# A planned attention and two-MLP kernel: who takes the head's maximum and the slope, which banks attention may use, and when the second weights are fetched

## The chip, the cores and the metric

The kernel runs on one core of a Trainium2 chip. The time is device microseconds of one execution. Three runs of the kernel before gave 874.43, 874.75 and 878.87 us; the median is 874.75 us. The engines have short names here: PE multiplies matrices (TensorE), DVE is VectorE, ACT is ScalarE, POOL is GpSimd, and SP issues most of the DMAs.

## The reference

Four batches of eight heads, 576 tokens and 64 dimensions go through linear attention with exponential features; the result, 2304 tokens by 512, goes through two MLPs of width 2048.

```python
def phi(x):                                   # x = q or k, scaled; omega is 128 x 64
    h = einsum('bhsd,md->bhsm', x, omega) - sum(x * x) / 2
    return exp(h - max(h, axis=-1)) / sqrt(m)
kv = einsum('bhsm,bhsd->bhmd', phi(k), v);  z = sum(phi(k), axis=2)
attn = einsum('bhsm,bhmd->bhsd', phi(q), kv) / (einsum('bhsm,bhm->bhs', phi(q), z) + 1e-6)
x = attn, heads side by side                  # 2304 x 512
h = x @ moe_w_in                              # 512 -> 2048
x = (maximum(h, 0) + alpha * minimum(h, 0)) @ moe_w_out
h = x @ moe2_w_in
x = where(h >= 1, h, where(h <= -1, 0, (h + 1)**2 / 4)) @ moe2_w_out
```

The term with x * x is the same for all features of a token, so the maximum that is subtracted takes it out again.

## The kernel before, in words

All work is written as Python generators. A planner (`Plan`, L38) runs them while the kernel is built: each step names an engine, a cost in ns and the instruction; where a step is a list, `_choice` (L105) takes the engine on which it would end first by the planner's costs, plus a handicap that the list may give. The step that can start first is emitted next. So the order on every engine is fixed when the program is built, and each engine goes through its queue in that order. Tokens stand for buffers and PSUM banks; a generator that asks for one waits until another gives it back.

Attention goes by pairs of heads: 16 pairs, four to a batch. For a pair, `features` (L527) multiplies keys and queries by omega into two PSUM banks, and `exponentials` (L503) takes for each head of a pair the maximum over the features on DVE and then the exponentials on ACT, in one of two ways. Either ACT runs one instruction of 128 columns for each of the four token blocks, with the maximum as its bias (L523); or DVE first subtracts the maximum from all 512 columns (L514), which frees the bank, and ACT runs one instruction of 512 columns (L516). In the kernel before, the second head of keys and of queries of pairs 0 to 5 (`N_SUB = 6`) goes the second way. `transposed` turns the query features on PE, `key_sums` forms kv, and the quotients end with a multiplication on POOL for the main 512 tokens and one for the remaining 64 (L805).

The first MLP works on batches 0 to 2 in 48 units, 16 of 128 hidden features for each batch. A unit is twelve matmuls of 512 columns into a hidden bank (h0 or h1), the slope, a split of the result into a high and a low part (`hi_of`, `lo_of`, L275 and L282), and twelve matmuls into the output banks y0 to y3. The order on PE is hidden of unit i + 1, then output of unit i, and attention of the later batches stands between. Before the first unit, batch 0 of attention must be done (four pairs) and x split; PE fills planned gaps of 600 ns and more there with matmuls on zeros (L1819, called fills here). Until the first hidden matmuls are in the queue, attention uses the banks y0 to y3, a0 and a1; then only a0 and a1.

The slope (L924 to L930) is two DVE instructions: t = min(h, 0) * alpha, then h = max(h, 0) + t, both reading the hidden bank. The weights arrive as 64 bit floats and are converted in five steps on ACT or POOL, ACT, DVE, DVE and POOL (`convert`, L311); then a high and a low part is made (`split`, L481): the high part on ACT, the low part by a subtraction on POOL or DVE. The second MLP's weights are fetched from unit 14 on (`W2_FROM`). From 376 us on the first MLP's last batch and the second MLP run in Strassen-like form, which the change does not touch.

Of the kernel before, what the change touches and what calls it, by code (L numbers as in the profile page):

```python
# [146 lines left out]
def _act(n, emit, more=0.0):  # L147
    return "act", 100 + 0.833 * n + more, emit


def _dve(n, emit, handicap=0.0):
    return "dve", 65 + 1.05 * n, emit, handicap
# [27 lines left out]
def favor_attention_two_mlps(  # L180
# [20 lines left out]
    nc = tc.nc  # L201
# [16 lines left out]
    NR = GT // P  # L218
    K2 = KC // 2
    AHEAD = 5  # L220
    N_SUB = 6
    SQ = 32
    BY_SQUARES = range(6, 16)
    ZW = 32
# [2 lines left out]
    WARM = 18  # L227
    WARM_NS = 125
    W2S = 4, 5
    W2_FROM = 14  # L230
    FRESH = 10
    SPLIT_EARLY = 4
    PACE = 0
# [31 lines left out]
    def ev(*key):  # L265
        return events.setdefault(key, Event())

    def done(*key):
        plan.set(ev(*key))
# [211 lines left out]
    def split(both, w):  # L481
        hi, lo = both[:, 0, :], both[:, 1, :]
        yield hi_of(hi, w, 3000)
        yield lo_of(lo, w, hi, ("pool", "dve2"), 600)


    free_banks = Tokens(["y0", "y1", "y2", "y3", "a0", "a1"])
    xs_of_pair, v_slots, split_slot = Tokens([0, 1]), Tokens([0, 1]), Tokens([0])
    k_slot = Tokens([0, 1])
    q_slot = Tokens([0])  # L490
# [6 lines left out]
    def give(tag):  # L497
        if tag[0] == "a" or not started:
            plan.put(free_banks, tag)
        else:  # L500
            plan.put(y_banks, tag)

    def exponentials(pool, pr, tag, dst, key):  # L503

        n = dst.shape[1]


        pv = pr[:, : n * M].rearrange("p (n m) -> p n m", m=M)
        nm = pool.tile([P, 4], F32, tag="nm", name="nm", bufs=8)[:, :n]
        yield _dve(n * M, lambda: nc.vector.tensor_reduce(nm, pv, AX.X, ALU.max, negate=True))  # L510
        if key[0] in ("k1", "q1") and key[1] < N_SUB:

            most = nm.unsqueeze(2).to_broadcast([P, n, M])
            yield _dve(n * M, lambda: nc.vector.tensor_tensor(dst, pv, most, ALU.add))  # L514
            give(tag)
            yield _act(n * M, lambda: nc.scalar.activation(dst, dst, AF.Exp), 10)  # L516
            done(*key)
            return
        for i in range(n):
            src = pv[:, i, :]  # L520
            if len(dst.shape) > 3:
                src = src.rearrange("p (c t) -> p c t", t=SQ)
            yield _act(M, lambda: nc.scalar.activation(dst[:, i], src, AF.Exp, bias=nm[:, i : i + 1]), 40)  # L523
        give(tag)
        done(*key)

# [244 lines left out]
    def inverted(pair):  # L771
        b, hp = divmod(pair, NP)
        den, num, inv, sums = backs[pair]
        yield ev("den", pair)
        squares = den.rearrange("p (s j) -> p s j", j=32)
        halves = inv.rearrange("p (i s) -> p i s", i=2)

        def add():
            nc.vector.tensor_scalar(sums, squares[:, NS // 2 :, 0], EPS, None, ALU.add)

        def invert():
            nc.vector.reciprocal(halves, sums.unsqueeze(1).to_broadcast([P, 2, NS // 2]))
# [12 lines left out]
        if pair in BY_SQUARES:  # L795
            o, a, r = ends[0]
            a, r = (e.rearrange("p (r j t) -> p r j t", j=NJ, t=SQ) for e in (a, r))
            ends[0] = o.rearrange("p (j r t) -> p r j t", j=NJ, t=SQ), a, r
        for i, (o, a, r) in enumerate(ends):
            for p in range(2):  # L800
                yield ev("num", pair, p)
            n = a.free_size()
            yield [
                _dve_two(n, lambda: nc.vector.tensor_tensor(o, a, r, ALU.mult), 2000),
                _pool(n, lambda: nc.gpsimd.tensor_tensor(o, a, r, ALU.mult)),  # L805
            ]
        plan.put(den_slot, 0)
        done("pair", pair)

# [79 lines left out]
    def attended():  # L889
        for b in range(B):  # L890
            for hp in range(NP):
                yield ev("pair", b * NP + hp)
            if b < B - 1:
                done("x", 0, b)
        att.close()
        late["pool"] = ctx.enter_context(tc.tile_pool(name="late", bufs=1, reuse_waits="tile"))
        late["zero"] = late["pool"].tile([P, 512], F32R, name="zero")
        nc.gpsimd.memset(late["zero"].bitcast(F32), 0.0)
        for u in range(2):
            late["g", u] = late["pool"].tile([P, 2, GT], F32R, name=f"g{u}")  # L900
        done("late")
        done("x", 0, B - 1)
        done("x", 0, B)
# [5 lines left out]
    def split_x(b, c):  # L909
# [7 lines left out]
        xs[c] = hi, lo  # L917
        done("xs", b, c)

    t_slots = Tokens([0])  # L920
    g_slots = Tokens(["g0", "g1"])
    gs = {}

    def activate(i, h, tag):  # L924
        g, f = units[i]
        yield t_slots
        t = moe_p.tile([P, SM], F32, tag="t", name="t")
        a = alpha_sb[:, f : f + 1]
        yield _dve(SM + 57, lambda: nc.vector.tensor_scalar(t, h, 0.0, a, ALU.min, ALU.mult))
        yield _dve(SM, lambda: nc.vector.scalar_tensor_tensor(h, h, 0.0, t, ALU.max, ALU.add))  # L930
        plan.put(t_slots, 0)
        tg = yield g_slots
        both = moe_p.tile([P, 2, SM], F32R, tag=tg, name="g")
        g_hi, g_lo = both[:, 0, :], both[:, 1, :]
        yield hi_of(g_hi, h)
        yield lo_of(g_lo, h, g_hi)
        plan.put(h_banks, tag)
        gs[i] = g_hi, g_lo, tg
        done("g", i)

    h_banks = Tokens(["h0", "h1"])
    y_banks = Tokens([])

    def hidden(i, c, h):
# [22 lines left out]
    def first_mlp():  # L967
        ys = {}
        for i in range(-1, NU):
            if i + 1 < NU:  # L970
# [16 lines left out]
                if not started:  # L987
                    started.append(1)
                    for at, tag in list(free_banks.free):
                        if tag[0] == "y":  # L990
                            free_banks.free.remove((at, tag))
                            y_banks.free.append((at, tag))
                if i + 1 == NU - 1:
                    done("first hidden")
            if i < 0:
# [85 lines left out]

    def second_parts(m, j):
        if not m:
            yield ev("unit", NF + 7 * j // 2)
        for u in range(2):
            yield ev("w", m, 2 * j + u, 0)
        rank = NU + 2 * j if m else NF + 2 * j
# [704 lines left out]
    ident = const.tile([P, P], F32, name="ident")  # L1792
    alpha_sb = const.tile([P, NF], F32, name="alpha_sb")
    half = const.tile([P, 1], F32, name="half")

    ctx.enter_context(tc.manual_schedule())
    att = ExitStack()
# [59 lines left out]
        yield "act", 300, constants  # L1857

    plan.add(setup(), URGENT)
    plan.add(load(alpha_sb, alpha, ("alpha",)), 0)  # L1860
    for f in range(-AHEAD, 0):
        done("unit", f)
    plan.add(attend(pool), 3, -10)
# [74 lines left out]
```

## Time and profile before

| | |
|---|---|
| median of three runs | 874.75 us |
| span of the profiled execution, first to last instruction | 872.5 us |
| PE busy | 862.4 us, 99% |
| DVE busy | 746.8 us, 86% |
| ACT busy | 547.1 us, 63% |
| POOL busy | 257.0 us, 29% |
| granted clock | 0.999 of 2.4 GHz over the span |
| first hidden matmul of the first MLP | 52.30 us |
| end of the first MLP's plain units | about 376 us |

The busy time of PE counts each matmul until its result has drained, so rows overlap: a matmul of 512 columns is shown with 0.39 us, while the next one starts 0.23 us behind it. Whether PE is late is therefore read from the starts of its rows and from its waits, not from the 99%. The number in brackets at a row of the timeline is the idle time ahead of it and what ended it.

### The profile page before, as it was taken

What the parts mean: (1) busy time and instruction counts of PE and PEld (TensorE: products, weight loads), DVE (VectorE), ACT (ScalarE), POOL (GpSimd) and SP (SyncE); (2) the same over time, 40 slices, a digit from 0 to 9 for tenths busy, and PEclk for the clock granted to TensorE, in tenths of its full rate; (3) what the DMA queues carried; (4) which work ended last, traced back from release to release, by engine and by line L of the source; (5) the groups of instructions that cost most, each with busy time, mean ns of one, the idle gap of its engine ahead of it and who ended that gap; (6) DMA issues with size and microseconds to landing.
All of it is one profiled execution on the core that took longest, in us unless ns stands there. A gap on an engine that the chain in (4) does not pass through costs nothing.

```text
span 872.5 us, 17520 instructions
## 1 busy us (share of the span) xinstructions
PE 862.4 (99%) x6197; PEld 758.7 (87%) x6197; DVE 746.8 (86%) x1385; ACT 547.1 (63%) x1193; POOL 257.0 (29%) x230
## 2 busy tenths in 40 slices
PE   8999999999999999999999999999999999999998
PEld 7777777777777788889999999989999999999998
DVE  6998998998886989898999999765978998688964
ACT  6996776676767654344755666655567765476653
POOL 1665667566759876200112012100000000000000
PEclk9999999999999999999999999999999999999999
DMA  9869978589999767779877769978487788888773
GB/s 241 232 195 262 261 216 249 188 282 288 314 327 333 242 203 270 268 262 310 283 266 251 267 208 317 322 265 289 157 293 255 277 260 253 251 270 241 234 244 127
DMA packets 122791, 224.05 MB, mean 257 GB/s; under 512 B 41936, under 2 KB 60496, under 8 KB 122704
## 3 DMA queue, kind: packets, MB, share of 16 engines
q1 hardware_dynamic: 122400, 222.74, 78.9%
q8 instruction: 49, 0.80, 0.4%
q14 instruction: 38, 0.31, 0.1%
q10 hardware_dynamic: 304, 0.20, 0.1%
HBM read 163.13 MB, written 59.77 MB: 255 GB/s over the span
## 4 chain that ended last, share of the span: by engine, by line
PE 86%; DMA 6%; ACT 2%; DVE 2%; issue 1%; SPq 1%; POOL 1%; ACTq 0%; DVEq 0%; POOLq 0%
PE y L293 12%; PE y L294 11%; PE y L295 11%; PE h L293 11%; PE h L295 11%; PE h L294 11%; PE a L295 4%; PE a L294 4%; PE a L293 4%; DMA raw<-w 3%; PE a L544 2%; PE a L711 2%; PE a L648 1%; PE y L544 1%; POOL w L336 1%
## 5 line engine op out<-in xcount | busy, mean ns | idle before, releaser
L336 POOL TENSOR_TENSOR w<-w,raw 128x512 uint32<-128x512 uint32 x64 | 97.2, 1526 | 233.9 <-DVE w L335 201.6
L293 PE MATMUL h<-x_hi,w_set 128*128 128x384 f32 x288 | 97.2, 338 | 0.0
L295 PE MATMUL h<-x_hi,w_set 128*128 128x384 f32 x288 | 96.9, 336 | 0.0
L294 PE MATMUL h<-x_lo,w_set 128*128 128x384 f32 x288 | 96.8, 336 | 0.0
L293 PE MATMUL y<-g,w_parts 128*128 128x512 f32 x192 | 78.0, 406 | 0.0
L293 PE MATMUL h<-x_hi,w_parts 128*128 128x512 f32 x192 | 77.3, 403 | 0.0
L295 PE MATMUL h<-x_hi,w_parts 128*128 128x512 f32 x192 | 75.1, 391 | 0.5 <-POOL w_parts L288 0.5
L294 PE MATMUL y<-g,w_parts 128*128 128x512 f32 x192 | 75.0, 391 | 0.0
L295 PE MATMUL y<-g,w_parts 128*128 128x512 f32 x192 | 75.0, 391 | 0.0
L294 PE MATMUL h<-x_lo,w_parts 128*128 128x512 f32 x192 | 74.8, 390 | 0.0
L288 POOL TENSOR_TENSOR w_parts<-w,w_parts 128x512 fp32r<-128x512 f32 x40 | 53.4, 1335 | 21.2 <-ACT w_parts L277 18.9
L277 ACT ACTIVATE g<-h 128x512 fp32r<-128x512 f32 x48 | 28.7, 598 | 47.2 <-DVE h L930 47.2
L293 PEld LDWEIGHTS h<-x_hi,w_set 128*128 128x128 f32 x288 | 54.1, 188 | 3.8 <-ACT e L1330 0.3
L294 PEld LDWEIGHTS h<-x_lo,w_set 128*128 128x128 f32 x288 | 54.1, 188 | 3.3
L277 ACT ACTIVATE g<-gates 128x384 fp32r<-128x384 f32 x72 | 37.6, 526 | 30.6 <-PE y L294 10.6
L295 PEld LDWEIGHTS h<-x_hi,w_set 128*128 128x128 f32 x288 | 54.1, 188 | 0.0
L331 DVE SCALAR_TENSOR_TENSOR raw<-raw 128x512 uint32<-128x512 uint32 x64 | 50.6, 801 | 1.2 <-issue 0.8
L287 DVE TENSOR_TENSOR g<-gates,g 128x384 fp32r<-128x384 f32 x72 | 39.4, 552 | 13.9 <-ACT g L277 13.6
L277 ACT ACTIVATE w_parts<-w 128x512 fp32r<-128x512 f32 x58 | 36.6, 633 | 21.7 <-PE h L295 10.5
L293 PEld LDWEIGHTS y<-g,w_parts 128*128 128x128 f32 x192 | 36.1, 188 | 9.5 <-PE a L711 0.5
L294 PE MATMUL y<-g,w_out 128*128 128x512 f32 (+1 forms) x120 | 44.1, 367 | 0.0
L295 PE MATMUL y<-g,w_out 128*128 128x512 f32 (+1 forms) x120 | 43.9, 366 | 0.0
(248 smaller groups left out, 2709.0 us busy)
## 6 DMA issues: line engine op xcount, KB each, us to landing
w_set<-w_kept SPq DMA_DIRECT2D x56, 512.0 KB, 5.3
w_out<-w_kept SPq DMA_DIRECT2D x56, 512.0 KB, 4.3
raw<-w SPq DMA_DIRECT2D x48, 512.0 KB, 5.5
w_kept<-w_keep SPq DMA_DIRECT2D x72, 256.0 KB, 4.0
w_set<-w_kept SPq DMA_DIRECT2D x24, 768.0 KB, 4.4
w_again<-w_word SPq DMA_DIRECT2D x48, 256.0 KB, 3.6
w_kept<-w_keep SPq DMA_DIRECT2D x24, 512.0 KB, 5.1
kq<-kq SPq DMA_DIRECT2D x15, 576.0 KB, 5.2
```

The lines of the kernel that those rows point to most:

```text
L277: ops = [_act(n, lambda: nc.scalar.activation(hi, src, AF.Copy))]
L287: "dve2": _dve_two(n, lambda: nc.vector.tensor_tensor(*args), bias),
L288: "pool": _pool(n, lambda: nc.gpsimd.tensor_tensor(*args)),
L293: nc.tensor.matmul(out_, wh, mh, start=first, stop=False, skip_group_check=more)
L294: nc.tensor.matmul(out_, wh, ml, start=False, stop=False, skip_group_check=more)
L295: nc.tensor.matmul(out_, wl, mh, start=False, stop=last, skip_group_check=more)
L331: lambda: nc.vector.scalar_tensor_tensor(low, e, 0x80000000, low, ALU.bitwise_and, ALU.bitwise_or),
L336: yield _pool(n, lambda: nc.gpsimd.tensor_tensor(d, d, low, ALU.add))
L544: nc.tensor.matmul(o, x[rows, c], om[rows, :], start=True, stop=True)
L648: nc.tensor.matmul(o, kf[:, 2 * j + h, r], vm[:, h, j, :], start=False, stop=end)
L711: nc.tensor.matmul(o[r], weights[i], moving[i], start=True, stop=True)
```

## The change

- `exponentials`: which of the two ways a head goes is no longer fixed for the second heads of pairs 0 to 5, but chosen by the planner for every head of four token blocks of pairs 0 to 3 (`N_SUB = 4`), the way over ACT alone with a handicap of 200.
- `slope` (new): the first of its two instructions may run on ACT (t = relu(-h)); then DVE forms h = h + t * (1 - alpha). The old two DVE instructions remain as the other choice. The table 1 - alpha (`rest_sb`) is made once, on POOL.
- `split`: the low part of the weights is made by DVE alone.
- Bank h1 belongs to attention until the first hidden matmuls are in the queue, and to the hidden units after that.
- The second weights are fetched from unit 10, and their sums are formed from unit 16 + 3j instead of 16 + 3.5j.
- A batch of x may be split when the main multiplication of its last pair is in the queue, ahead of that for the remaining 64 tokens.

```diff
-    N_SUB = 6
+    N_SUB = 4
-    W2_FROM = 14
+    W2_FROM = 10
@@ split
-        yield lo_of(lo, w, hi, ("pool", "dve2"), 600)
+        yield lo_of(lo, w, hi, ("dve2",))
@@
-    free_banks = Tokens(["y0", "y1", "y2", "y3", "a0", "a1"])
+    free_banks = Tokens(["y0", "y1", "y2", "y3", "a0", "a1", "h1"])
@@ give
-            plan.put(y_banks, tag)
+            plan.put(y_banks if tag[0] == "y" else h_banks, tag)
@@ exponentials
-        if key[0] in ("k1", "q1") and key[1] < N_SUB:
-            most = nm.unsqueeze(2).to_broadcast([P, n, M])
-            yield _dve(n * M, lambda: nc.vector.tensor_tensor(dst, pv, most, ALU.add))
+        first = _act(M, lambda: one(0), 40)
+        if n == NJ and key[1] < N_SUB:
+            yield [(*first, 200), ("dve", 65 + 1.05 * n * M, take)]
+        else:
+            yield first
+        if taken:
             give(tag)
             yield _act(n * M, lambda: nc.scalar.activation(dst, dst, AF.Exp), 10)
@@ inverted
+            done("pair", pair, i)
@@ attended
-                yield ev("pair", b * NP + hp)
+                yield ev("pair", b * NP + hp, 0)
@@ activate
-        yield _dve(SM + 57, lambda: nc.vector.tensor_scalar(t, h, 0.0, a, ALU.min, ALU.mult))
-        yield _dve(SM, lambda: nc.vector.scalar_tensor_tensor(h, h, 0.0, t, ALU.max, ALU.add))
+        yield from slope(h, t, f)
@@ slope, new
+        def relu():
+            nc.scalar.activation(t, h, AF.Relu, scale=-1.0)
+        def leaky():
+            nc.vector.scalar_tensor_tensor(h, t, rest, h, ALU.mult, ALU.add)
+        yield [
+            (*_act(SM, relu), 0),
+            _dve(SM + 57, lambda: nc.vector.tensor_scalar(t, h, 0.0, a, ALU.min, ALU.mult)),
+        ]
+        if on_act:
+            yield _dve(SM + 57, leaky)
+        else:
+            yield _dve(SM, lambda: nc.vector.scalar_tensor_tensor(h, h, 0.0, t, ALU.max, ALU.add))
@@
-    h_banks = Tokens(["h0", "h1"])
+    h_banks = Tokens(["h0"])
@@ second_parts
-            yield ev("unit", NF + 7 * j // 2)
+            yield ev("unit", NF + 3 * j)
```

What the planner makes of it, counted over the whole program: of 48 units 41 take the slope's first step on ACT; of 12 heads that DVE subtracted before, 3 remain; the subtractions for w_parts<-w go from 40 on POOL and 18 on DVE to 58 on DVE; the fills go from 25 matmuls to 17, besides the 18 at the start. Besides that, a few conversions and sums change engines.

On PE, around the first hidden unit, the queue before reads as follows. The number behind a name tells buffers apart, the letter and digit ahead of it is the PSUM bank; warm_w is a fill, qf, kf, lf are features of a pair, qt and kvz the two operands of the quotients, and h0_1194 is unit 0.

```order
L1819 MATMUL h0_214<-warm_w_208 128x256 x8
L677 MATMUL y3_1107<-ident_196,qf_1022 128x128 x4
L711 MATMUL y0_1123<-qt_875,kvz_919 32x288 x4
L711 MATMUL a1_1122<-qt_875,kvz_919 32x512 x4
L711 MATMUL y0_1123<-qt_875,kvz_919 32x64 x4
L642 MATMUL y0_1123<-vl1_240,lf_876 32x130 x4
L648 MATMUL y0_1123<-vm1_239,kf_879 32x65 x32
L677 MATMUL y2_1190<-ident_196,qf_1022 128x128 x4
L293 MATMUL h0_1194<-x_hi_1114,w_parts_731 128x512
```

The same place now, from the last three matmuls of unit 0 (h0_1128) to the first three of unit 1 (h0_1238):

```order
L293 MATMUL h0_1128<-x_hi_1090,w_parts_599 128x512
L294 MATMUL h0_1128<-x_lo_1091,w_parts_599 128x512
L295 MATMUL h0_1128<-x_hi_1090,w_parts_599 128x512
L723 MATMUL h1_1158<-qt_895,kvz_964 32x288 x4
L723 MATMUL a0_1157<-qt_895,kvz_964 32x512 x4
L723 MATMUL h1_1158<-qt_895,kvz_964 32x64 x4
L654 MATMUL h1_1158<-vl1_241,lf_896 32x130 x4
L660 MATMUL h1_1158<-vm1_240,kf_900 32x65 x32
L689 MATMUL a1_1170<-ident_196,qf_1058 128x128 x4
L293 MATMUL h0_1238<-x_hi_1084,w_parts_918 128x512
L294 MATMUL h0_1238<-x_lo_1085,w_parts_918 128x512
L295 MATMUL h0_1238<-x_hi_1084,w_parts_918 128x512
```

Unit 0 stands ahead of the block of attention behind which it stood, the eight fills ahead of that block are gone, and units 0 and 1 use the same bank, since attention still has h1.

On ACT, the queue before around the high part of unit 0 (g_1322):

```order
L523 ACTIVATE kf_1211<-a0_1254,nm_1272 128x128
L523 ACTIVATE kf_1211<-y1_1255,nm_1273 128x128
L277 ACTIVATE g_1322<-h0_1194 128x512
L523 ACTIVATE kf_1211<-a0_1254,nm_1272 128x128
L523 ACTIVATE kf_1211<-y1_1255,nm_1273 128x128
```

And now, from ACT's last exponential ahead of the slope of unit 0 (t_1166) to its high part (g_1225); raw is a weight in conversion:

```order
L522 ACTIVATE qf_1058<-a1_1062,nm_1078 128x128
L327 ACTIVATE raw_1045<-raw_1045 128x512
L939 ACTIVATE t_1166<-h0_1128 128x512
L277 ACTIVATE w_parts_1167<-w_253 128x512
L522 ACTIVATE lf_1060<-y0_1066,nm_1097 128x128
L522 ACTIVATE kf_1064<-y3_1103,nm_1116 128x128
L277 ACTIVATE g_1225<-h0_1128 128x512
```

The unit's chain now passes ACT twice. Between ACT's first split of x for unit 0 (x_hi_1084) and t_1166 there stand one more split of x, thirteen exponentials and three steps on raw.

On DVE, the queue before around the slope of unit 0 (t_1292, h0_1194):

```order
L929 TENSOR_SCALAR t_1292<-h0_1194,alpha_sb_197 128x512
L331 SCALAR_TENSOR_TENSOR raw_732<-raw_732 128x512
L930 SCALAR_TENSOR_TENSOR h0_1194<-h0_1194,t_1292 128x512
L560 STREAM_TRANSPOSE qf_1208<-qf_1208 128x512
L335 TENSOR_SCALAR w_255<-raw_732 128x512
L929 TENSOR_SCALAR t_1330<-h1_1294,alpha_sb_197 128x512
L286 TENSOR_TENSOR g_1322<-h0_1194,g_1322 128x512
```

And now, around the same slope:

```order
L287 TENSOR_TENSOR w_parts_1044<-w_257,w_parts_1044 128x512
L331 SCALAR_TENSOR_TENSOR raw_600<-raw_600 128x512
L943 SCALAR_TENSOR_TENSOR h0_1128<-t_1166,rest_sb_199,h0_1128 128x512
L287 TENSOR_TENSOR w_parts_1167<-w_253,w_parts_1167 128x512
L286 TENSOR_TENSOR g_1225<-h0_1128,g_1225 128x512
```

One DVE instruction of the slope has gone to ACT, and two subtractions for weights have come from POOL.

## Rows read from the trace of the kernel before

**Rows 1.** The page: span, and busy time of each engine.

```profile
span 872.5 us, 17520 instructions
PE 862.4 (99%) x6197; PEld 758.7 (87%) x6197; DVE 746.8 (86%) x1385; ACT 547.1 (63%) x1193; POOL 257.0 (29%) x230
```

**Rows 2.** Stretches: length, busy PE, PEld, DVE, ACT, POOL; clock, DMA share, GB/s.

```profile
5.00:48.80 43.80, 42.09 (x751) 31.54 (x752) 40.11 (x90) 38.49 (x112) 20.41 (x21) 1.00 0.93 236
...
57.00:100.00 43.00, 41.25 (x378) 31.67 (x378) 39.58 (x68) 31.72 (x80) 28.13 (x23) 1.00 0.86 257
...
300.00:376.00 76.00, 76.00 (x340) 61.97 (x339) 68.05 (x101) 33.18 (x57) 40.35 (x34) 1.00 0.71 242
376.00:580.00 204.00, 203.52 (x1113) 187.77 (x1112) 187.35 (x367) 122.75 (x236) 24.48 (x15) 1.00 0.81 277
580.00:873.00 293.00, 289.18 (x1770) 282.73 (x1769) 228.77 (x443) 173.32 (x356) 1.27 (x1) 1.00 0.74 242
```

**Rows 3.** Waits of PE: what waited for what: us in total, times, longest.

```profile
PE a L679 <- ACT qf L523: 1.3, 2, 0.9
...
PE a L711 <- ACT kf L523: 0.9, 1, 0.9
...
PE a L544 <- ACT lf L523: 0.6, 1, 0.6
PE h L295 <- POOL w_parts L288: 0.5, 1, 0.5
PE y L293 <- DMA w_out<-w_kept: 0.5, 1, 0.5
```

**Rows 4.** Timeline of PE around the first hidden unit, and in steady state.

```profile
47.23 1.21 PE L1819 MATMUL h<-warm_w 128*128 128x256 f32 x8
48.57 0.66 PE L677 MATMUL y<-ident,qf 128*128 128x128 f32 x4
49.16 0.69 PE L711 MATMUL y<-qt,kvz 128*32 128x288 f32 x8
...
51.89 0.66 PE L677 MATMUL y<-ident,qf 128*128 128x128 f32 x4
52.30 0.47 PE L293 MATMUL h<-x_hi,w_parts 128*128 128x512 f32 x1
...
302.02 0.40 PE L293 MATMUL h<-x_hi,w_parts 128*128 128x512 f32 x1
302.25 0.39 PE L294 MATMUL h<-x_lo,w_parts 128*128 128x512 f32 x1
```

**Rows 5.** Timeline of ACT ahead of the first hidden unit.

```profile
9.67 0.63 ACT L516 ACTIVATE kf<-kf 128x512 f32<-128x512 f32 x1 [0.43 <-DVE kf L514]
...
23.91 0.37 ACT L523 ACTIVATE qf<-y,nm 128x128 f32<-128x128 f32 x1 [1.19 <-DVE nm L510]
...
48.90 0.65 ACT L277 ACTIVATE x_hi<-x 128x512 fp32r<-128x512 f32 x1
...
50.15 0.41 ACT L523 ACTIVATE kf<-y,nm 128x128 f32<-128x128 f32 x1
50.40 0.42 ACT L523 ACTIVATE kf<-a,nm 128x128 f32<-128x128 f32 x1
```

**Rows 6.** Groups by line: shapes, count | busy us, mean ns | idle before, by whom.

```profile
L929 DVE TENSOR_SCALAR t<-h,alpha_sb 128x512 f32<-128x512 f32 x48 | 35.5, 739 | 6.7 <-PE h L295 6.7
...
L287 DVE TENSOR_TENSOR w_parts<-w,w_parts 128x512 fp32r<-128x512 f32 x18 | 18.4, 1029 | 0.1
...
L514 DVE TENSOR_TENSOR kf<-y,nm 128x512 f32<-128x512 f32 x3 | 2.1, 687 | 0.1
...
L277 ACT ACTIVATE g<-h 128x512 fp32r<-128x512 f32 x48 | 28.7, 598 | 47.2 <-DVE h L930 47.2
...
L327 ACT ACTIVATE raw<-raw 128x512 uint32<-128x512 uint16 x64 | 43.5, 680 | 0.0
```

**Rows 7.** Instructions on w_parts: count: duration ns least/median/most, first and last start.

```profile
L288 POOL TENSOR_TENSOR w_parts<-w,w_parts x40: 1271/1298/1754, 32.1 to 322.0; 128x512 fp32r<-128x512 f32 x40
...
L287 DVE TENSOR_TENSOR w_parts<-w,w_parts x18: 675/692/1804, 32.0 to 334.3; 128x512 fp32r<-128x512 f32 x18
```

More of the change, by code (lines that the diff above doesn't have):

```diff
@@ L510, in exponentials, with take, one @@
         yield _dve(n * M, lambda: nc.vector.tensor_reduce(nm, pv, AX.X, ALU.max, negate=True))
-        if key[0] in ("k1", "q1") and key[1] < N_SUB:
-            most = nm.unsqueeze(2).to_broadcast([P, n, M])
-            yield _dve(n * M, lambda: nc.vector.tensor_tensor(dst, pv, most, ALU.add))
+        most = nm.unsqueeze(2).to_broadcast([P, n, M])
+        taken = []
+        def take():
+            nc.vector.tensor_tensor(dst, pv, most, ALU.add)
+            taken.append(1)
+        def one(i):
+            src = pv[:, i, :]
+            if len(dst.shape) > 3:
+                src = src.rearrange("p (c t) -> p c t", t=SQ)
+            nc.scalar.activation(dst[:, i], src, AF.Exp, bias=nm[:, i : i + 1])
+        first = _act(M, lambda: one(0), 40)
[4 more added lines that the diff above has]
+        if taken:
             give(tag)
@@ L518, in exponentials @@
             return
[L519 to L523, printed above, removed]
+        for i in range(1, n):
+            yield _act(M, lambda: one(i), 40)
         give(tag)
@@ L891, in attended @@
             for hp in range(NP):
-                yield ev("pair", b * NP + hp)
+                yield ev("pair", b * NP + hp, 0)
             if b < B - 1:
                 done("x", 0, b)
+        for pair in range(B * NP):
+            yield ev("pair", pair)
         att.close()
@@ L918, in split_x, with slope @@
         done("xs", b, c)
+    def slope(h, t, f):
+        a, rest, on_act = alpha_sb[:, f : f + 1], rest_sb[:, f : f + 1], []
+        def relu():
+            nc.scalar.activation(t, h, AF.Relu, scale=-1.0)
+            on_act.append(1)
+        def leaky():
[8 more added lines that the diff above has]
+            yield _dve(SM, lambda: nc.vector.scalar_tensor_tensor(h, h, 0.0, t, ALU.max, ALU.add))
     t_slots = Tokens([0])
@@ L927, in activate @@
         t = moe_p.tile([P, SM], F32, tag="t", name="t")
-        a = alpha_sb[:, f : f + 1]
-        yield _dve(SM + 57, lambda: nc.vector.tensor_scalar(t, h, 0.0, a, ALU.min, ALU.mult))
-        yield _dve(SM, lambda: nc.vector.scalar_tensor_tensor(h, h, 0.0, t, ALU.max, ALU.add))
+        yield from slope(h, t, f)
         plan.put(t_slots, 0)
@@ L989, in first_mlp @@
                     for at, tag in list(free_banks.free):
-                        if tag[0] == "y":
+                        if tag[0] != "a":
                             free_banks.free.remove((at, tag))
-                            y_banks.free.append((at, tag))
+                            (y_banks if tag[0] == "y" else h_banks).free.append((at, tag))
                 if i + 1 == NU - 1:
@@ L1794, in favor_attention_two_mlps @@
     half = const.tile([P, 1], F32, name="half")
+    rest_sb = const.tile([P, NF], F32, name="rest_sb")
     ctx.enter_context(tc.manual_schedule())
@@ L1859, in favor_attention_two_mlps, with slopes @@
     plan.add(setup(), URGENT)
-    plan.add(load(alpha_sb, alpha, ("alpha",)), 0)
+    def slopes():
+        yield from load(alpha_sb, alpha, ("alpha",))
+        args = rest_sb, alpha_sb, -1.0, 1.0, ALU.mult, ALU.add
+        yield "pool", 200, lambda: nc.gpsimd.tensor_scalar(*args)
+    plan.add(slopes(), 0)
     for f in range(-AHEAD, 0):
```

## The prediction

> **What bounds the kernel now.** I read the page first. PE is busy for 99% of 872.5 us, DVE for 86%, ACT for 63% [rows 1]. The 99% alone says little, since a row of PE lasts until its result has drained, so I went on to the stretches and to PE's waits. Behind 300 us PE is full: 76.00 of 76.00 us, then 203.52 of 204.00 [rows 2]; only the tail of the program shows a gap. In steady state one matmul of 512 columns starts 0.23 us behind the other [rows 4], so a unit's twelve hidden matmuls take 2.7 us, and nothing of the change makes a matmul shorter. The time can therefore move only where PE stands or is filled: 0.48 us of wait at most behind 300 us, some waits in the first 155 us, and the fills ahead of the first unit. The waits that matter are 1.3, 0.9 and 0.6 us for ACT, 0.5 us for a subtraction of weights on POOL, and 0.5 us for a DMA [rows 3]; the eight fills last from 47.23 to 48.57, 1.3 us [rows 4]. That is 5.1 us, and it is about what a perfect change could give. There is much more room on the other side.
>
> The runs' median of 874.75 us is 2.25 us above the profiled span. I add the steps to the median, as if what lies around the span stays.
>
> **First unit.** Equal work has to be compared. When unit 1 begins now, PE has done unit 0, the block of attention, and four of the eight transposes. Before, the block and all eight transposes were done at 52.30; without four transposes (0.59 us, 48.57 to 49.16) and with unit 0's 2.7 us that is 54.4 us [rows 4].
>
> Now for the same point in the new order. ACT's first split of x began at 48.90. Ahead of it ACT stood 0.43 and 1.19 us waiting for DVE [rows 5]. Up to there ACT's queue now has 23 exponentials more, at the 0.25 us between two starts [rows 5] 5.8 us; nine of 512 columns less, at some 0.5 us (a row of 0.63 less the overlap) 4.5 us; and two exponentials for the last rows and two raw steps less, 1.6 us, against some small copies more: even, within half a us. DVE has nine subtractions of 0.69 us less there, 6.2 us [rows 6], so I take 1.5 of the 1.62 us as gone: x_hi begins at 47.4 and ends at 47.9, x_lo follows at 0.69 us and a hop, and unit 0 starts at 48.7. PE then has 2.7 us of unit 0, 2.73 of the block (49.16 to 51.89) and 0.59 of transposes: it reaches unit 1 at 54.7. But unit 1 needs bank h0 back, and that hangs on ACT: from 47.9 one more split (0.5), thirteen exponentials (3.25), three raw steps (0.57 each without overlap, 1.7), relu (0.5), a weight and two exponentials (1.0), the high part (0.6, [rows 6]) and DVE's low part with its hop (0.8) make 8.35 us. The bank is free at 56.3. That is 1.9 us behind 54.4, although the fills are gone: **+1.9 us**. Bounds: with none of ACT's waits gone +3.5 us; with the bank in time only the fills count, -1.3 us.
>
> **Exponentials and slope, behind the first unit.** On DVE: 41 first steps of the slope less at 0.74 us (30.3), nine subtractions less (6.2), forty subtractions of weights more at 0.69 us (27.6) [rows 6, 7]: 8.9 us less over some 320 us. On ACT 41 relu more. The trace has no relu of 128x512 out of a bank; the nearest row is the high part with 0.60 us, 0.5 without overlap [rows 6]: 21 to 25 us more. ACT was busy for 31.7 of 43 us between 57 and 100 [rows 2], some six units, so 5.3 us a unit become 5.8 of 7.2. There is room, and I cost the relu itself at nothing; were ACT full, each would cost PE 0.5 us. What it does to PE's waits is open. Three of them end with late exponentials, whose maxima come from DVE; a lighter DVE helps, a longer ACT queue hurts. Between all gone (-2.8 us) and twice as long (+2.8 us) I take two thirds gone, because in these rows ACT is held up by DVE more than by its own work: its high part of a unit alone stood 47.2 us for DVE, 1.0 us a unit [rows 6]. **-1.9 us.**
>
> **Subtractions for weights.** PE's one wait of 0.5 us for POOL goes: **-0.5 us**. Whether it comes back on DVE depends on how long they take there. DVE's own row says 0.69 us in the median, 1.80 at most and 1.03 in the mean, while POOL's take 1.30 [rows 6, 7]: some of DVE's are held for 1.1 us. The Trainium skill ("SBUF — State Buffer", section "Who interferes with whom") says that a DVE instruction with two inputs in SBUF and a GpSimd instruction that reads SBUF exclude each other for the whole instruction. The spread of the 18 rows agrees with it. By that rule the forty moved ones are held as the 18 are, for POOL keeps its 64 other additions: forty at 1.03 us are 41.2 us, and DVE's sum turns from -8.9 to +4.7 us. I stay with the median, since 52 us of POOL's work leave with them; the other sum is a rival below.
>
> **Second weights, the early split, the table.** Fetching from unit 10 moves conversions and sums into a stretch in which POOL has just lost 52 us. PE shows no wait on these weights, and DMA is at a share of 0.71 to 0.86 [rows 2]: nothing. If that cover fails, the loss is of the size of the one DMA wait, 0.5 us a time; I keep -0.5 to +1.5 us. The early release of x saves POOL's short multiplication on x's path, but ACT's place in its queue decides there, as above. The table is one small POOL instruction: nothing.
>
> **Sum:** +1.9 - 1.9 - 0.5 = -0.5, so 874.75 becomes 874.2 us.
>
> **Rivals.**
> - *DVE's relief reaches PE.* The bank is in time, the fills are pure gain (-1.3), and the ACT waits and the POOL wait all go (-3.3): 870.1 us. For it: DVE was busy for 40.1 of 43.8 us before the split [rows 2]. Against it: the bank needs ACT 2 us earlier than its queue allows.
> - *ACT becomes the bound (slower).* The place is ACT's queue from unit 0 on. None of its waits goes, unit 1 starts 3.5 us late, and since every unit passes ACT twice, it stands twice a unit for DVE or PE; the exponentials come later and PE's ACT waits double (+2.8), less 0.5: 880.5 us. A unit lasts 7.2 us; 5.8 of work and 1.0 of standing leave 0.4. It decides once the standing grows past 1.4 us a unit. For it: the chain now crosses engines once more. Against it: the slope on DVE gets shorter.
> - *DVE is held by POOL.* DVE's sum grows, the ACT waits stay, and a late weight stops PE three times at 0.5 us instead of once: +1.9 + 1.0 = 877.7 us. The rule of the Trainium skill speaks for it. Against it: one wait in forty subtractions before.
> - *It does little of what it says.* Three heads still go over DVE and bank h1 serves attention for the first 50 us alone; what ACT loses at unit 1 the fills give back: 874.7 us.
>
> **How the numbers follow.** About 0.5%, 4.4 us, is what a measurement tells from no change. Chances: the forecast 0.37, DVE's relief 0.20, ACT 0.20, held DVE 0.08, little 0.15. The forecast's own range is 871.5 to 877. Faster by over 0.5% (under 870.4 us) takes 0.12 of the relief, which lies at that edge, and 0.04 of the forecast: 0.16. Slower (over 879.1) takes 0.16 of ACT, 0.02 of held DVE and 0.03 of the forecast: 0.21. The rest is 0.63. The range reaches over the relief and nearly over ACT: 869 to 880.
>
> **What would show it.** In the profile after: unit 0 starts near 48.7 and unit 1 near 56.3, with a wait of PE of about 1.6 us for DVE's low part of g; PE's waits for ACT behind that sum to about 1 us; DVE's busy time falls by some 9 us, ACT's rises by 25, POOL's falls by 50; behind 300 us PE stays full. A unit 1 that starts at 54.5 without a wait speaks for the relief; waits of PE at most units for ACT's exponentials speak for ACT; DVE subtractions with a mean of 1 us speak for the lock. New waits of PE behind 300 us, or a stretch of PE there that isn't full, would overthrow the whole account.

## The result, and the profile after

The changed kernel takes 886.36 us (median of 6 runs, 884.62 to 889.62), the kernel before 874.71 beside it (6 runs): a ratio of 1.0134, 95% interval 1.0115 to 1.0152, or 11.65 us more. That is slower, and above the upper end of the predicted range. The profiled execution has a span of 886.5 us.

The page of the changed kernel, span and busy times, against [rows 1]:

```profile
span 886.5 us, 17489 instructions
PE 868.1 (98%) x6189; PEld 761.5 (86%) x6189; DVE 738.8 (83%) x1376; ACT 567.7 (64%) x1255; POOL 208.4 (24%) x196
```

The work moved nearly as forecast: DVE 8.0 us less (9 forecast), ACT 20.6 more (25), POOL 48.6 less (50). The time did not come from work. PE's waits in the changed kernel, the largest, against [rows 3] (what waited for what: us in total, times, longest):

```profile
PE a L723 <- ACT kf L522: 6.5, 2, 6.3
PE a L599 <- DMA kq<-kq: 3.2, 1, 3.2
...
PE h L294 <- DVE x_lo L287: 0.6, 1, 0.6
PE h L293 <- DVE g L286: 0.5, 1, 0.5
```

Two waits are new. The larger one is at 270 us, in a part of the program that the prediction gave no row of: [rows 2] leave out 100 to 300 us. Stretches around it in the changed kernel, columns as in [rows 2] (length, busy PE, PEld, DVE, ACT, POOL; clock, DMA share, GB/s):

```profile
260.00:270.00 10.00, 10.00 (x55) 7.86 (x54) 5.17 (x8) 3.88 (x9) 7.00 (x7) 1.00 0.99 343
270.00:277.00 7.00, 0.73 (x9) 0.27 (x12) 2.18 (x3) 3.75 (x10) 0.73 (x2) 0.86 0.40 154
277.00:282.00 5.00, 5.00 (x97) 3.18 (x90) 0.14 (x1) 0.59 (x1) 1.27 (x1) 0.51 0.52 161
...
300.00:376.00 76.00, 76.00 (x526) 59.81 (x525) 71.93 (x113) 50.97 (x103) 41.27 (x36) 1.00 0.83 274
376.00:580.00 204.00, 203.61 (x1101) 186.04 (x1101) 184.96 (x354) 116.07 (x222) 20.91 (x14) 1.00 0.83 275
```

Up to 270 PE is full and the DMA engines too, at 0.99. Then PE stands, and after it the granted clock is 0.51: near 1.2 of its 2.4 GHz, the lower of its two levels. Behind 300 us PE is full, as forecast. PE's timeline there (start, length, operation, wait and releaser):

```profile
269.79 0.39 PE L295 MATMUL h<-x_hi,w_parts 128*128 128x512 f32 x1
276.45 3.11 PE L723 MATMUL a<-qt,kvz 128*32 128x288 f32 x24 [6.27 <-ACT kf L522]
279.33 0.66 PE L654 MATMUL a<-vl,lf 128*32 128x130 f32 x8
279.77 1.96 PE L660 MATMUL a<-vm,kf 128*32 128x65 f32 x64
281.65 0.62 PE L293 MATMUL h<-x_hi,w_parts 128*128 128x512 f32 x1
```

The last matmul ahead of the stop starts at 269.79, and the next could have followed at 270.02, 0.23 us later. PE stands 6.4 us, and the block of attention from 276.45 to 281.65 takes 5.2 us where the same block took 2.73 at full clock [rows 4]. Together 8.9 us. What ACT did, from its timeline:

```profile
265.52 0.60 ACT L939 ACTIVATE t<-h 128x512 f32<-128x512 f32 x1
273.17 0.63 ACT L277 ACTIVATE w_parts<-w 128x512 fp32r<-128x512 f32 x1 [7.05 <-DMA w_kept<-w_parts]
273.70 0.61 ACT L522 ACTIVATE kf<-a,nm 128x128 f32<-128x128 f32 x2
```

ACT was not busy: it stood 7.05 us at a split of first weights, and the exponentials that PE needed stood behind it in ACT's queue. The split waits for a store. Its slot holds the parts of two weights ahead (as the buffers' names in the program tell), and those had not yet been read out to `w_kept`. DVE's low part for that slot, and SP's queue behind it:

```profile
250.25 0.91 DVE L287 TENSOR_TENSOR w_parts<-w,w_parts 128x512 fp32r<-128x512 f32 x1
```

```profile
259.00 2.62 SPq L584 DMA_DIRECT2D q_kept<-qf  x4
261.67 1.97 SPq L1170 DMA_DIRECT2D w_kept<-w_keep  x2
...
264.85 0.93 SPq L1170 DMA_DIRECT2D w_kept<-w_parts  x1
265.88 0.58 SPq L589 DMA_DIRECT2D qt<-q_kept  x1
266.51 2.23 SPq L1170 DMA_DIRECT2D w_kept<-w_parts  x2
```

The parts were ready at 251.2; the second of their two stores was issued at 266.51, 15.3 us later, behind stores of features and of second weights, and ACT went on when it had landed, 21.9 us behind the parts. In the kernel before, POOL made the low part for the same slot, and the second of its two stores was issued 0.9 us behind the parts and had landed after 4.9:

```profile
254.81 1.28 POOL L288 TENSOR_TENSOR w_parts<-w,w_parts 128x512 fp32r<-128x512 f32 x1 [0.37 <-ACT w_parts L277]
```

```profile
256.52 1.34 SPq L1138 DMA_DIRECT2D w_kept<-w_parts  x2
```

Other stores of parts were later there too: one was issued 6.9 us behind its parts, and another landed 12.4 us behind them. No instruction waited for one.

The code shows how this can be. `first_mlp` gives the slot back to the plan as soon as PE has read the parts by the planner's reckoning (`plan.put(part_slots[0], ...)`), and the stores are added with a late rank, `NU` (48). The plan may therefore set ACT's next split into that slot ahead of a store which it has put off. The result stays right, since the split waits for the store. ACT pays for it with its whole queue.

The smaller new wait is at the start. PE's timeline of the changed kernel, against [rows 4]:

```profile
21.80 0.33 PE L691 MATMUL y<-ident,lf 128*128 128x128 f32 x1
25.30 0.67 PE L599 MATMUL a<-om_two,kq 128*128 128x256 f32 x2 [3.16 <-DMA kq<-kq]
...
51.51 0.49 PE L293 MATMUL h<-x_hi,w_parts 128*128 128x512 f32 x1
...
59.24 0.50 PE L293 MATMUL h<-x_hi,w_parts 128*128 128x512 f32 x1 [0.50 <-DVE g L286]
```

Unit 0 starts at 51.51 (48.7 forecast) and unit 1 at 59.24 (56.3), both 2.8 to 2.9 us behind the forecast, after a wait of 3.16 us for keys and queries.

### The profile page after: what moved, and what is told of

It reads as the page before. It is cut to its first block, busy times and chain, and to the rows that moved or that the text cites. A ratio compares the mean times of both kernels' runs of the same rounds, so it can differ in the third digit from the quotient of the medians.

```text
span 886.5 us, 17489 instructions
## 1 busy us (share of the span) xinstructions
PE 868.1 (98%) x6189; PEld 761.5 (86%) x6189; DVE 738.8 (83%) x1376; ACT 567.7 (64%) x1255; POOL 208.4 (24%) x196
## 4 chain that ended last, share of the span: by engine, by line
PE 81%; DVE 7%; ACT 4%; DMA 4%; issue 1%; SPq 1%; POOL 0%; ACTq 0%; DVEq 0%; POOLq 0%
PE y L293 11%; PE y L294 11%; PE y L295 11%; PE h L293 10%; PE h L295 10%; PE h L294 10%; PE a L295 4%; PE a L294 4%; PE a L293 4%; DMA raw<-w 2%; PE a L556 2%; PE a L723 2%; DVE w_parts L287 1%; PE a L660 1%; ACT kf L522 1%
## 5 line engine op out<-in xcount | busy, mean ns | idle before, releaser
L336 POOL TENSOR_TENSOR w<-w,raw 128x512 uint32<-128x512 uint32 x64 | 93.0, 1456 | 256.9 <-DVE w L335 200.2
L287 DVE TENSOR_TENSOR w_parts<-w,w_parts 128x512 fp32r<-128x512 f32 x58 | 47.6, 823 | 11.1 <-ACT w_parts L277 10.7
L331 DVE SCALAR_TENSOR_TENSOR raw<-raw 128x512 uint32<-128x512 uint32 x64 | 48.3, 762 | 3.1 <-ACT raw L327 2.5
L293 PEld LDWEIGHTS h<-x_hi,w_parts 128*128 128x128 f32 x192 | 36.1, 188 | 10.8 <-DVE g L286 0.7
L327 ACT ACTIVATE raw<-raw 128x512 uint32<-128x512 uint16 x64 | 44.7, 698 | 0.3 <-DMA raw<-w 0.3
```

Source lines behind the costliest of these rows:

```text
L287: "dve2": _dve_two(n, lambda: nc.vector.tensor_tensor(*args), bias),
L293: nc.tensor.matmul(out_, wh, mh, start=first, stop=False, skip_group_check=more)
L327: yield _act(n, lambda: nc.scalar.activation(low, h, AF.Copy, scale=2.0**-13), 35)
L331: lambda: nc.vector.scalar_tensor_tensor(low, e, 0x80000000, low, ALU.bitwise_and, ALU.bitwise_or),
L336: yield _pool(n, lambda: nc.gpsimd.tensor_tensor(d, d, low, ALU.add))
```

## The experiments

Theory A, in its first form: the early second weights fill the DMA engines, a store of parts comes late, and ACT stands behind it. Rivals: any other order does the same (B), ACT's longer queue is too slow (C). Four kernels undid one part each.

```
e1:  W2_FROM = 14;  yield ev("unit", NF + 7 * j // 2)
e2:  yield lo_of(lo, w, hi, ("pool", "dve2"), 600)
e3:  N_SUB = 6, DVE by rule; free_banks without "h1"; the event of a whole pair
e5:  slope: yield _dve(SM + 57, ...min, mult...); no relu on ACT
```

Second weights late again (e1): 

> The changed kernel with the second weights fetched from unit 14 and summed from 16 + 3.5j again; all else as changed. The queue of PE is the same up to row 585, so the first 100 us are the same. Theory A (the long stop of PE at 270 us, 6.4 us and 2.5 us at half clock, comes from the second weights being fetched earlier, which fills the DMA rings while a store of weight parts is under way): that stop goes, the 3.2 us wait for kq at 21.8 us stays: 877 to 880 us. Rival B (the stop comes from the order of stores and splits, which any of the new steps brings about): the stop or another of its size stays: 884 to 888 us.

Subtractions open to POOL again (e2): 

> The changed kernel with the weights' subtraction on POOL or DVE again, as before. The first 84 rows of PE are the same, so the wait for kq at 21.8 us stays in both theories. Theory A: the second weights still come early, the stop near 270 us stays: 884 to 888 us. Rival B: with the splits of weights in other places the stop is not there: 877 to 880 us.

Heads and banks of before (e3): 

> The changed kernel with attention as before: second heads of pairs 0 to 5 over DVE, h1 for the hidden units only, the whole pair awaited. PE's queue is that of the kernel before up to row 119. Theory A: the wait for kq (3.2 us, with some 1.5 us at a lower clock behind it) goes, the stop near 270 us stays: 879 to 882 us. Rival C (the loss comes from ACT's longer queue, with relu, all along): 884 us or more.

Slope on DVE (e5): 

> The changed kernel with the slope as two DVE instructions, as before. PE's queue is the same up to row 174, the wait for kq stays. Theory A: the stop near 270 us stays, DVE has some 27 us more to do: 884 to 889 us. Rival C (ACT's queue with relu): 41 relu less, the stop for ACT goes: 877 to 880 us.

| kernel | median us | ratio to before, 95% | waits of ACT for a store of parts, of 2 us or more |
|---|---|---|---|
| e1 | 877.62 | 1.0028 [1.0009, 1.0047] | none |
| e2 | 883.20 | 1.0104 [1.0075, 1.0134] | none |
| e3 | 887.38 | 1.0142 [1.0098, 1.0186] | 7.07 and 3.01 |
| e5 | 885.87 | 1.0123 [1.0098, 1.0149] | 4.84 |

ACT's timelines of e3 (two rows) and of e5 (one):

```profile
256.47 0.63 ACT L277 ACTIVATE w_parts<-w 128x512 fp32r<-128x512 f32 x1 [7.07 <-DMA w_kept<-w_parts]
273.40 0.63 ACT L277 ACTIVATE w_parts<-w 128x512 fp32r<-128x512 f32 x1 [3.01 <-DMA w_kept<-w_parts]
```

```profile
276.17 0.63 ACT L277 ACTIVATE w_parts<-w 128x512 fp32r<-128x512 f32 x1 [4.84 <-DMA w_kept<-w_parts]
```

e1 spoke for A, but e2 has early second weights and no such stop, and e3 has it twice and missed A's figure. Against C, e5 has no relu on ACT and is as slow as the changed kernel. So the next four asked whether the lateness lies in the plan's order, by changing only how the plan treats the stores (f1, f2), and what each of two parts does alone in the kernel before.

```
f1:  plan.add(store_kept(kept[0, j, k], both, ...), URGENT)     # NU before; the rest of a store likewise
f2:  plan.add(free_part(i + 1), URGENT)                         # was plan.put(part_slots[0], ...)
     free_part: yield ev("stored", 0, j, k) for each store of these parts, then plan.put
```

> The changed kernel, with one thing different: the stores of first-weight parts (w_kept<-w_parts) get the planner's first rank (-10) instead of the last (48), so SP issues them sooner. Theory A (the long stop comes from a store that stands late in SP's order, here 15.3 us behind the parts, while the planner has already given the part slot back; ACT then stands at the head of its queue for that slot): no wait of ACT on w_kept<-w_parts above 2 us, stores issued at most 6 us behind their parts, clock 1.00 in 260 to 290 us, time 876 to 880 us, like the version with late second weights (877.6). Rival D (the DMA engines are full and any order leaves a store late): the stop stays, moved, and the time is 884 to 889 us.

> The changed kernel, with one thing different: the planner gives a part slot back only when the store of the parts has landed in its own reckoning, instead of when PE has read them. Theory A: ACT's split is planned behind the store, so the exponentials stand ahead of it in ACT's queue; no wait of ACT on w_kept<-w_parts above 3 us; 876 to 881 us. Rival D (DMA engines full, order does not matter): parts come late instead, PE waits for them, 884 to 889 us. If the planner's own reckoning of a store is far too early, the stop stays at 884 to 888 as well, with the wait still on ACT: that would be a third reading, and it is seen on the waits.

> The kernel before with only the second weights fetched from unit ten and their sums spread at three units instead of three and a half; attention, slope, splits and banks as before. If the early second weights alone make the stop: a wait of ACT on w_kept<-w_parts of 4 us or more behind 240 us and 880 to 886 us. If it takes the early second weights and the subtractions on DVE together (the version with both sorts of subtraction had no such stop in its trace): 874 to 877.5 us and no such wait.

> The kernel before with only the subtractions for weights given to DVE alone; all else as before. By the prediction's own terms: PE's 0.5 us of waiting for POOL goes, DVE gets 27.6 us more work in 300 us: 874 to 877 us. By the rival that DVE is held by POOL: some waits of PE for w_parts on DVE, 877 to 879 us. If the subtractions alone bring the stop behind a store: 880 us and more, with a wait of ACT on w_kept<-w_parts of 4 us or more.

| kernel | median us | ratio to before, 95% | waits of ACT for a store of parts, of 2 us or more |
|---|---|---|---|
| f1 | 879.89 | 1.0062 [1.0039, 1.0084] | none |
| f2 | 878.23 | 1.0038 [1.0016, 1.0060] | none |
| b_w2_only | 880.15 | 1.0063 [1.0037, 1.0090] | none |
| b_split_only | 889.69 | 1.0169 [1.0132, 1.0205] | 7.78 and 2.25 |

f1 and f2 change no instruction's work, only the order: PE's is that of the changed kernel for about 200 us and another behind that. The long stop is gone, and 6.5 and 8.1 of 11.65 us come back. That falls as A's expectation had it, and D (full DMA engines, whatever the order) falls with it. In f2 the same stretches are full, at full clock, with the DMA engines at 0.93 to 0.95:

```profile
260.00:270.00 10.00, 10.00 (x139) 7.64 (x139) 8.45 (x16) 5.26 (x15) 2.81 (x3) 1.00 0.94 311
270.00:277.00 7.00, 7.00 (x42) 5.22 (x42) 6.67 (x12) 6.17 (x17) 0.81 (x1) 1.00 0.93 288
277.00:282.00 5.00, 5.00 (x24) 4.12 (x23) 4.83 (x9) 5.00 (x15) 0.09 (x1) 1.00 0.95 279
```

b_w2_only is 5.6 us slower without such a stop, which neither reading of its expectation had. Its PE has the order of the kernel before for over 100 us, and yet in its profile the first unit starts at 55.93, against 52.30. The surprise is the last kernel: the subtractions on DVE alone, with late second weights, bring the stop by themselves. ACT's timeline of it, and three stretches:

```profile
262.36 0.63 ACT L277 ACTIVATE w_parts<-w 128x512 fp32r<-128x512 f32 x1 [7.78 <-DMA w_kept<-w_parts]
```

```profile
255.00:262.00 7.00, 7.00 (x42) 5.40 (x40) 3.96 (x9) 0.00 (x0) 3.94 (x4) 1.00 0.92 323
262.00:268.00 6.00, 1.88 (x5) 1.36 (x5) 3.37 (x4) 5.64 (x16) 3.51 (x5) 0.77 0.46 138
268.00:275.00 7.00, 7.00 (x27) 5.30 (x27) 4.27 (x8) 3.19 (x7) 5.24 (x6) 0.71 0.78 253
```

So A's first form was too narrow. Neither early second weights nor these subtractions are needed for the stop (s2 below has one of 3.46 us with neither): a plan that frees a slot with its store still open meets it wherever the new order happens to put that store late. Four kernels with f2's edit tested this on other parts.

> The kernel before with the subtractions for weights on DVE alone (889.7 us by itself) and a part slot that the planner gives back only when its store has landed. Theory A (the whole cost of that edit is a store behind which ACT stands, not DVE's work): 875 to 880 us, no wait of ACT on w_kept<-w_parts above 2 us, clock 1.00 in 260 to 280 us. Rival (DVE's extra 27.6 us, or its being held by POOL, is what costs): 886 to 890 us.

> The changed kernel with the subtractions open to POOL again (883.2 us by itself, without a stop behind a store in its trace) and the held slot. Theory A has nothing to take away here: 881 to 885 us. If it falls to 876 to 880, the held slot does more than remove that stop, by another order of the whole middle.

> The changed kernel with the heads and the attention banks of before (887.4 us by itself, two stops behind stores in its trace) and the held slot. Theory A: the stops go, 875 to 880 us. If heads and banks are what costs the rest (the changed kernel with the held slot has 878.2), it comes to 874 to 876; if they gain something, 879 to 882. Rival (some other cost of early weights): 884 to 888.

> The changed kernel with the slope as two instructions on DVE (885.9 us by itself) and the held slot. Theory A: 876 to 881 us. If ACT's part of the slope is worth what the prediction took for it (two thirds of 2.8 us), this is 1 to 3 us slower than the 878.2 of the changed kernel with the held slot; if ACT's longer queue costs, it is faster by as much.

| kernel | median us, without and with the held slot | ratio to before, 95% (held) |
|---|---|---|
| g1, subtractions alone | 889.69, 880.70 | 1.0055 [1.0025, 1.0084] |
| g2, change with POOL | 883.20, 881.55 | 1.0066 [1.0045, 1.0087] |
| g3, change with old heads | 887.38, 879.22 | 1.0045 [1.0031, 1.0060] |
| g4, change with slope on DVE | 885.87, 891.89 | 1.0187 [1.0166, 1.0208] |

In none does ACT stand 2 us for a store of parts. Where the stop had been long (g1, g3) 8 to 9 us come back; where there was none (g2), 1.6. g1 stays 0.7 us above A's range. There PE waits 1.8 us in two for DVE's subtractions, where it had waited 0.5 for POOL; the longer wait:

```profile
126.88 0.51 PE L295 MATMUL h<-x_hi,w_parts 128*128 128x512 f32 x1 [1.56 <-DVE w_parts L287]
```

g4 missed: the stop is gone and the time is worse. From 364 to 376 us DVE is full there, with one subtraction of 2.57 us among its rows, and PE waits 3.1 us in two for g and then runs at a lower clock:

```profile
367.57 2.57 DVE L287 TENSOR_TENSOR x_lo<-x,x_hi 128x768 fp32r<-128x768 f32 x1
```

```profile
364.00:370.00 6.00, 5.02 (x22) 4.18 (x23) 6.00 (x7) 4.23 (x7) 1.85 (x1) 1.00 1.04 398
370.00:376.00 6.00, 4.00 (x14) 2.88 (x13) 5.96 (x10) 0.60 (x1) 0.00 (x0) 0.83 0.43 161
```

In that order DVE is the bound for a while. PE's longest wait in g4, 3.6 us for ACT's split of weights at 149 us, was there without the held slot too (3.1 us in e5). The rest of g4's loss stays open.

Left over were the 3 to 4 us of f2 and e1. Four kernels took parts of the change without the others, all with late second weights:

```
s1: slope by either engine.   s2: heads, bank h1 and the half-pair event.
s3: slope and subtractions on DVE.   s4: heads, bank and slope, subtractions as before.
```

> The kernel before with only the slope by either engine. By the prediction: DVE loses up to 48 first steps of 0.74 us, PE's waits for late exponentials shrink by up to 2.8 us: 872 to 874.5 us. If ACT's longer queue costs instead, 876 to 879 us with more waits of PE for ACT.

> The kernel before with only the exponentials by plan, bank h1 lent to attention and the event per half pair. By the prediction's first term: +1.9 us, 876 to 878 us, if unit 1 has to wait for bank h0. If this part is where the remaining 3 to 4 us are: 877.5 to 880 us. If not: 873 to 875 us.

> The kernel before with the slope by either engine and the subtractions on DVE alone, nothing else. If the subtractions cost only where DVE is full, and the slope on ACT makes room for them: 873 to 876 us (the subtractions alone, with the held slot, had 880.7). If the remaining 3 to 4 us are theirs: 877.5 to 880 us. With a long stop behind a store, which nothing in the order speaks for: 884 to 889 us.

> The changed kernel without its early second weights and with the subtractions open to POOL as before: heads, bank and slope stay. If the remaining 3 to 4 us belong to heads and bank: 877 to 880 us. If they belong to the subtractions: 873 to 875.5 us.

s1 878.60 us (1.0045 [1.0031, 1.0060]), s2 881.34 (1.0090 [1.0055, 1.0124]), s3 884.93 (1.0100 [1.0068, 1.0132]), s4 881.13 (1.0067 [1.0041, 1.0093]). s2 and s4 are slower than any branch of their expectations. s1 falls into its branch "ACT's longer queue", but without that branch's sign: PE waits 2.6 us for ACT there, 3.4 in the kernel before. s3 falls into the branch of a stop behind a store, for which I had seen nothing in the order. s2 and s3 do have the stop again, 3.46 us at 290 and 4.00 us at 270. The row of s3:

```profile
269.55 0.63 ACT L277 ACTIVATE w_parts<-w 128x512 fp32r<-128x512 f32 x1 [4.00 <-DMA w_kept<-w_parts]
```

No single part holds the rest: alone, the slope costs 3.5 us, the early second weights 5.6, the subtractions with the slot held 5.5, and the heads 6.2 with their stop in it; all of them together, with the slot held, cost 3.6. The parts do not add up.

The last two: the held slot in the kernel before, and both ways of treating the stores together.

> The kernel before with only the held slot: the planner gives a part slot back when its store has landed. No store of parts was later than 5.8 us there and ACT stood for none, so Theory A has nothing to remove: 873.5 to 876.5 us. If it is 3 us or more slower, a good part of what f2 kept over the kernel before is the mend's own; if faster, the mend is a gain by itself.

> The changed kernel with both mends: stores of parts at the planner's first rank, and the slot held until they land. Theory A: no stop of ACT behind such a store; 876 to 880 us, as with either alone (879.9 and 878.2). Below 874 it would beat the kernel before, for which nothing speaks but the 1.7 us by which the held version stood ahead at the last hidden unit in its profile.

v2 takes 875.62 us beside 875.62 (0.9996 [0.9979, 1.0013]): the mend alone costs and gains nothing (one store stood 6.9 us behind its parts there, not 5.8 at most as I had written). That fits the reading that what f2 gave back is the stop's price; but PE's order in v2 is that of the kernel before, so it does not show what the new order of a mended plan costs or gains by itself. v1 takes 882.52 (1.0083 [1.0056, 1.0110]) and missed: it has no such stop, but PE waits 3.1 us for kq, 2.5 for `num` and 1.0 for qt. No version beat the kernel before.

Over all the changed orders the waits of 2 us or more for a store of parts and the times go together in the main. Without one lie eleven kernels from 877.6 to 883.2 us; with 3.46, 4.00, 4.84, 7.05, 10.1 (in two) and 10.0 (in two) come 881.3, 884.9, 885.9, 886.4, 887.4 and 889.7. The two groups overlap, and each wait is that of one profiled execution beside the median of several. g4 is the exception; v2 keeps nearly the order of the kernel before.

## Why the prediction was wrong

- **The step that failed** is "Second weights, the early split, the table": "PE shows no wait on these weights, and DMA is at a share of 0.71 to 0.86 [rows 2]: nothing", with a bound of 1.5 us. With these weights late again (e1) the changed kernel loses 8.7 of its 11.65 us; in the kernel before they cost 5.6 us alone, without a long stop (b_w2_only). The step looked at the wrong stretches and asked the wrong question. Rows that I did not show, from the kernel before, between those of [rows 2]:

```profile
200.00:240.00 40.00, 40.00 (x375) 30.94 (x375) 34.80 (x65) 28.93 (x73) 27.27 (x26) 1.00 0.95 309
240.00:260.00 20.00, 20.00 (x193) 15.37 (x192) 17.36 (x31) 12.69 (x33) 10.98 (x12) 1.00 1.00 326
260.00:280.00 20.00, 20.00 (x194) 15.41 (x193) 13.29 (x25) 13.52 (x34) 16.75 (x17) 1.00 0.96 333
```

  The stop lies there, and there the DMA engines were at 0.95 to 1.00 before the change. Full engines alone do not make it, as f2 shows. The step did not ask who waits for a store: that a wait was absent before was taken for a cover, where it was luck of the order. With the stop went 8.1 us by f2, 8.9 by the trace. The same lies in the opening of the prediction, "The time can therefore move only where PE stands or is filled": no term of the sum stood for a wait that a new order makes. The late store landed 6.6 us after its issue; that is less than half of its 21.9 us, and the larger part was its place in SP's queue. In the changed kernel three stores of parts issued from 159 to 171 us, with the DMA engines at 0.56 to 0.78 until they landed, took 2.6 to 2.7 us; nine with the engines at 0.94 or more took 3.9 to 7.7; others do not fit (2.5 us at 0.86, 4.9 at 0.71). The Trainium skill ("DMA: Bandwidth & Descriptors", section "Latency and other measured facts") says that memory answers later under high load. The trace leans that way, but no run tells memory's answer from the wait for a busy DMA engine.
- **Subtractions for weights**, "-0.5 us": the wait for POOL did go, but alone the edit costs 5.5 us without the stop (g1), 1.8 of them PE's waits for the same subtractions on DVE, and 15 with it. In the whole change the moved subtractions were cheap: DVE's group reads

```profile
L287 DVE TENSOR_TENSOR w_parts<-w,w_parts 128x512 fp32r<-128x512 f32 x58 | 47.6, 823 | 11.1 <-ACT w_parts L277 10.7
```

  which is 29.2 us more than the 18 before [rows 6], 0.73 us for each of forty: 27.6 forecast. The rival of DVE held by POOL, 41.2 us, is refuted here in its size, though its mechanism is there. Of the 58 the 25 that began while a POOL instruction ran took 1.01 us in the mean and up to 1.80; the 33 others took 0.68, none over 0.69. These rows agree with the rule of the Trainium skill that the rival rested on ("SBUF — State Buffer", section "Who interferes with whom"). The rival took the mean of 18 rows, 9 of them begun so and held longer (1.38 us), for all forty.
- **First unit**, "+1.9 us": the mechanism is there, PE does wait for g at unit 1, but the size is off. f2, profiled in a run without the early wait, starts unit 0 at 46.66 and unit 1 at 54.41:

```profile
46.66 0.49 PE L293 MATMUL h<-x_hi,w_parts 128*128 128x512 f32 x1
...
54.41 0.50 PE L293 MATMUL h<-x_hi,w_parts 128*128 128x512 f32 x1 [0.74 <-DVE g L286]
```

  That is the 54.4 that I had for equal work, so in this execution the term is 0. From unit 0 to unit 1 are 7.75 us where 7.6 were forecast: ACT's sum held. What was off is the start of unit 0, 2 us earlier than the 48.7 that I took; which of the counts ahead of it was off stays open. It also varies: with the same order of PE up to there, e1 starts its units at 48.80 and 56.55, nearly as forecast, but behind a wait of 1.8 us that the forecast did not have. In the changed kernel's own profile the wait of 3.16 us, and the clock of 0.74 behind it, cover this.
- **Waits of PE**, "-1.9 us": in f2 PE's waits behind 60 us sum to 2.3 us, against 3.8 of [rows 3]. 1.5 us less, of 2.4 forecast with the POOL term: the right way, and some two thirds of the size, once the stop is out.
- **ACT becomes the bound** gave 880.5, on the right side, for another reason. ACT stood less, not more: 11.9 us at the high part of g, nearly all for DVE, where it had stood 47.2 [rows 6], and 19.3 at the new relu, for PE. PE did not wait at most units.
- **"New waits of PE behind 300 us, or a stretch not full, would overthrow the whole account":** the account fell to a wait ahead of 300 us, which the sentence left out.

**What stays open** is the rest of f2 and e1, 3.6 and 2.8 us where the forecast was 0.5 us faster. Two waits vary between profiles of the same order of PE. One is near 22 us, ahead of a matmul on keys and queries (kq): 3.16 us in the change, 1.44 in f1, none in f2, and 1.76 in e1, where the profile puts it down to ACT. Unit 0 then starts at 51.51, 49.19, 46.66 and 48.80. The kernel before has no wait for kq there, while b_w2_only, whose PE has the same order for over 100 us, shows 2.4. The changed kernel's profile and f2's thus reach unit 0 4.85 us apart, more than the rest; but they are single executions, the one among the slower of its kernel (888.53 beside a median of 886.36), the other among the faster (875.43 beside 878.23). The second wait is that of a matmul at 88 us for ACT's `num`, 0.3 to 2.5 us, behind ACT rows that stand for a load of raw weights. f1 there, ACT's row and the two stretches:

```profile
84.09 0.66 ACT L324 ACTIVATE raw<-raw 128x512 f32<-128x512 f32 x1 [3.32 <-DMA raw<-w]
```

```profile
84.00:88.00 4.00, 2.38 (x17) 1.61 (x9) 2.66 (x8) 3.43 (x7) 0.96 (x1) 1.00 1.11 315
88.00:92.00 4.00, 3.48 (x21) 2.86 (x22) 3.92 (x9) 2.27 (x5) 1.18 (x2) 0.70 1.07 179
```

Whether these make up the rest in the median was not shown: no experiment took either of them away.

## What to carry to other kernels

Before you cost a new order at nothing, list for each buffer who must have read it before it is written again, the DMA stores among them, and how late each may come; a wait that the profile does not show has a margin, and the margin is what the change spends. An engine that takes its queue in order turns one late store into a stop of all that stands behind it, so a planner should count the store as holding the slot: that took 8 to 9 us off three of the four kernels with a stop, and left the fourth slower (g4). Show rows for the stretch in which the change acts, not only for those at its sides.

## What the runs showed of the hardware

After a stop of PE of 2 to 6 us the granted clock was lower for some us more: 0.51 in 277 to 282 us of the changed kernel (6.4 us of standing), 0.77 and 0.71 in b_split_only, 0.70 in f1 behind a wait of 2.1 us, 0.83 in g4 behind waits of 1.1 and 2.0 us. The block behind the longest stop took 5.2 instead of 2.73 us, so that stop cost 2.5 us more than its length. Stores of parts, of 256 or 512 KB, landed 2.5 us after their issue at best and 7.7 at worst in the changed kernel. Of the changed kernel's 58 subtractions for weights on DVE, those begun while no POOL instruction ran took 0.68 us in the mean, the others 1.01.
